# How the first batch's q and k reach the chip: fp32 loads through SyncE and ScalarE, and transposes of two heads at once

## The chip, the cores and the metric

The kernel runs on one core of a Trainium2 chip. The metric is the device time of one execution in microseconds (us); several executions are measured and their median is given. The profile is of one execution, and its "span" is the time from the first to the last instruction in the trace.

The engines are called by their short names: PE (TensorE, the matrix multiplier; "PEld" are its weight loads), DVE (VectorE), ACT (ScalarE), POOL (GpSimd) and SP (SyncE, which only issues transfers here). Each engine works through its own instructions in order. Transfers (DMA) are issued from the queues of POOL, SP or ACT.

## The reference

Sliding-window attention with a linear bias by distance, and behind it a gated feed-forward block. Batch 8, 8 heads, 576 positions, head dimension 64; the inputs are fp32.

```python
scores = scale * np.matmul(q, k.transpose(0, 1, 3, 2))
slopes = 2.0 ** (-8.0 * (np.arange(H) + 1) / H)
bias = slopes[:, None, None] * (-np.abs(rel))[None, :, :]
mask = (rel >= 0) & (rel < 128)
scores = np.where(mask, scores + bias[None], -1e9)
attn = softmax(scores); attn_out = np.matmul(attn, v)
x = attn_out.transpose(0, 2, 1, 3).reshape(B * S, H * D)
out = (gelu(x @ w_gate) * (x @ w_val)) @ w_out
```

## The kernel before, in words

The 4608 tokens go through the feed-forward block in 9 groups of 512 (`gate_val` L465, `out_part` L493); the attention of batch b + 2 is spread over the steps of group g (`todo`, `steps`, L661 to L686). The order on each engine is that of the code. Batches 2 to 7 load q, k and v as bf16 through POOL's queue and are transposed by DMA. Batches 0 and 1 are transposed by PE, since they must be ready early.

**Batch 0** is a prologue written out by hand (L601 to L650).

The loads. `load_runs` (L137) loads q and k so that each partition holds r neighbouring positions of a head (r = 3 for positions 0 to 383, the "first part", on 128 partitions; and for 384 to 575, the "last rows", on 64 partitions, q on partitions 0 to 63 and k on 64 to 127 of one tile, `vb[1]`). The transfers convert fp32 to bf16 on the way and go through POOL's queue. L528 issues heads 0 to 3 of the first part (q, then k), L530 an iota that fills `tmpl` with key minus query distances, L532 heads 4 to 7, L533 the last rows, then v and the weights. POOL has eight completion counters for its transfers, so the ninth waits until the first has landed.

The tables. From `tmpl` DVE makes `ident` (L550, the identity for the transposes), `far` (L552), `tmpl` as distances (L554), `dist` in bf16 (L555), and `slopes` (L561, the identity times each head's slope, in two halves). ACT makes `emask` (L557, eight exps of 128x256, one for each head: the decay by distance); DVE copies parts of it to make the masks of the last blocks (`masks_of_last_blocks`, L578). `sel0`, `sel` and `sel8` select rows to spread the denominators, `ones4` and `ones8` sum them.

The work. `keep_busy(64)` puts 64 matmuls of zeros on PE ahead of the first real one. `first` (L590) transposes two heads of the first part: `transpose_runs` (L151) makes six transposes, one head and 64 columns each, and `untangle` (L162) copies the PSUM result to `qT` or `kT` in the order of positions. `biases0` and `scores0` (L254, L263) add slope times distance and q times k in PSUM, and ACT takes the exp (L209) into P. `rest` (L595) does the same for the last rows, in 12 transposes of 64x64 per call; `scores0_rest` (L273) makes their scores. `sums4` (L340) sums P by head (L364) and takes the reciprocal (L368); `products_first` and `spread_first` (L451, L456) multiply P with v (L431), spread the reciprocals (L378) and write `xT` (L459). `masks` are the products of P with `emask` (L212) that the last rows still need. Then `gate_val` (L473 matmuls, L479 gelu, L480 product) starts, with `sums4(0, 1)`, `spread4` and `values(0, 1)` between.

The buffers that the change uses: `wo`, the output matrix (12 slices of 512 columns), is loaded only at L651, and before that its slices 0 to 2 hold `slopes` and `dist`. The place of the last rows in `vb[1]` is that of batch 1's v, loaded at L654.

Of the kernel before, what the change touches and what calls it, by code (L numbers as in the profile page):

```python
# [7 lines left out]
FP32 = mybir.dt.float32  # L8
BF16 = mybir.dt.bfloat16
AF = mybir.ActivationFunctionType  # L10
# [22 lines left out]
def kernel(  # L33
# [30 lines left out]
    psum = ctx.enter_context(  # L64
        tc.tile_pool(name="psum", bufs=8, space=bass.MemoryType.PSUM))


    heat = [0]

    def bank():  # L70
        ps = psum.tile([128, 512], FP32, name="ps")
        for _ in range(heat.pop()):
            nc.tensor.matmul(out=ps[:, 0:64], lhsT=zeros, rhs=zeros[:, 0:64], start=True, stop=True)
        heat.append(0)
        return ps

    def keep_busy(n):
        heat[0] = n

    wg = consts.tile([128, 4, DFF], BF16, name="wg")  # L80
    wv = consts.tile([128, 4, DFF], BF16, name="wv")
# [55 lines left out]
    def load_runs(b, n, h0, h1):  # L137
        first, parts, r = RUNS[b][n]
        for what, src in ((0, q), (1, k)):
            nc.gpsimd.dma_start(  # L140
                out=runs(what, b, n)[:, h0:h1, :],
                in_=src[b][h0:h1, first:first + parts * r, :].rearrange(
                    "h (p r) d -> p h (r d)", r=r))
# [7 lines left out]
    def transpose_runs(b, n, what, c, ps):  # L151
        first, parts, r = RUNS[b][n]
        src = runs(what, b, n)
        p = 64 * what if (b, n) == (0, 1) else 0
        for x in range(r):
            for i in (0, 1):
                nc.tensor.transpose(  # L157
                    out=ps[64 * i:64 * i + 64, parts * x:parts * x + parts],
                    in_=src[:, 2 * c + i, 64 * x:64 * x + 64],
                    identity=ident[p:p + parts, p:p + parts])  # L160
# [93 lines left out]
    def biases0(cs):  # L254
        pss = []
        for c in cs:
            ps = [bank(), bank()]
            pss.append(ps)
            for i in (0, 1):
                bias(2 * c + i, ps[i], 2)  # L260
        return pss

    def scores0(cs, pss):  # L263
        for c, ps in zip(cs, pss):
            for j, q0, col in ((0, 0, 0), (1, 128, 256)):
                for i in (0, 1):
                    added(c, i, j, q0, 256, ps[i][:, col:col + 256])
        for c, ps in zip(cs, pss):
            for i in (0, 1):
                exp(prob(0)[:, c, i, 0:512], ps[i])  # L270


    def scores0_rest(cs, later):  # L273
        pss = []
        for c in cs:
            ps = [bank(), bank()]
            pss.append(ps)
            for j, q0, n, col in ((2, 384, 128, 0), (3, 384, 192, 128), (4, 512, 64, 320)):
                for i in (0, 1):
                    score(0, c, i, j, q0, n, ps[i][:, col:col + n])  # L280
        P = prob(0)
        for c, ps in zip(cs, pss):
            for i in (0, 1):
                exp(P[:, c, i, 640:1024], ps[i][:, 0:384])
            later.append((P[:, c, :, 640:1024], emask[:, 2 * c:2 * c + 2, 128:512]))
# [38 lines left out]
    def row(b):  # L324
        if b not in sumrow:
            sumrow[b] = r_pool.tile([128, S], FP32, name="r")
            recip[b] = r_pool.tile([128, 4, S], FP32, name="rb")
        return sumrow[b]
# [11 lines left out]
    def sums4(b, s, added=True):  # L340
        first, w, count = shape(b, s)
        ps = bank()
        P, T = prob(b).rearrange("p c i n -> p (c i) n"), both.get(b)
        mms = []
        for h in range(H):
            for x in range(count):
                t = first + w * x
                g, lhsT = ((x, ones4[:, 32 * h:32 * h + 32]) if count == 4 else
                           (2 * x + h // 4, ones8[:, 32 * (h % 4):32 * (h % 4) + 32]))
                if added and t >= 128:  # L350
                    mms.append((g, lhsT, T[:, h, t - 128:t - 128 + w], 0, w))
                elif added:
                    mms.append((g, lhsT, P[:, h, t:t + w], 0, w))
                else:
                    for _, a, e, col in PIECES[min(b, 1)][s]:
                        lo, hi = max(a, t), min(e, t + w)
                        if lo < hi:
                            mms.append((g, lhsT, P[:, h, col + lo - a:col + hi - a],
                                        lo - t, hi - t))

        by_group = [[m for m in mms if m[0] == g] for g in range(4)]
        mms = [ms[n] for n in range(max(map(len, by_group))) for ms in by_group if n < len(ms)]
        for n, (g, lhsT, rhs, lo, hi) in enumerate(mms):
            nc.tensor.matmul(  # L364
                out=ps[32 * g:32 * g + 32, lo:hi], lhsT=lhsT, rhs=rhs,
                start=all(m[0] != g for m in mms[:n]), stop=all(m[0] != g for m in mms[n + 1:]),
                skip_group_check=True)
        nc.vector.reciprocal(row(b)[:, first:first + w], ps[:, 0:w])  # L368
# [82 lines left out]
    def products_first(cs, copies):  # L451
        n = PARTS[0][0][1]
        for c, ps in zip(cs, products(0, 0, cs)):
            copies[c](out=recip[0][:, c, 0:n], in_=ps[:, 0:n])

    def spread_first():  # L456
        w = PARTS[0][0][1] // 4
        for g, ps in enumerate(spread4_banks(0, 0)):
            nc.vector.tensor_tensor(  # L459
                out=xT[:, :, w * g:w * g + w], in0=recip[0][:, :, w * g:w * g + w],  # L460
                in1=ps[:, 0:4 * w].rearrange("p (c x) -> p c x", c=4), op=ALU.mult)
# [63 lines left out]
    tmpl = consts.tile([128, 256], FP32, name="tmpl")  # L525
    far = consts.tile([128, 256], FP32, name="far")
    nc.vector.memset(zeros, 0.0)
    load_runs(0, 0, 0, 4)  # L528

    nc.gpsimd.iota(tmpl, pattern=[[1, 256]], base=0, channel_multiplier=-1,  # L530
                   allow_small_or_imprecise_dtypes=True)
# [9 lines left out]
        nc.vector.memset(slope1[:, h:h + 1], -8.0 * 2.0 ** (-8.0 * (h + 1) / H))  # L541
    nc.vector.memset(ones4, 0.0)
    nc.vector.memset(ones4.rearrange("p (h x) -> p h x", x=36)[:, :, 0:4], 1.0)
    nc.vector.memset(ones8, 0.0)
    nc.vector.memset(ones8.rearrange("p (h x) -> p h x", x=40)[:, :, 0:8], 1.0)
    for t in (kT[0], kT[1]):
        nc.vector.memset(t[:, :, 576:640], 0.0)
    for t in vb:
        nc.vector.memset(t[64:128, 4, :], 0.0)
    nc.vector.tensor_single_scalar(out=ident, in_=tmpl[:, 0:128], scalar=0.0, op=ALU.is_equal)  # L550
    for lo, bound, op in ((0, 0.0, ALU.is_lt), (128, 127.5, ALU.is_gt)):
        nc.vector.tensor_scalar(out=far[:, lo:lo + 128], in0=tmpl[:, lo:lo + 128],  # L552
                                scalar1=bound, scalar2=1e9, op0=op, op1=ALU.mult)
    nc.vector.tensor_tensor(out=tmpl, in0=tmpl, in1=far, op=ALU.max)  # L554
    nc.vector.tensor_copy(out=dist, in_=tmpl)  # L555
    for h in range(H):
        nc.scalar.activation(out=emask[:, h, 0:256], in_=tmpl, func=AF.Exp,  # L557
                             scale=-(2.0 ** (-8.0 * (h + 1) / H)))

    def made_slopes(lo, hi):  # L560
        nc.vector.tensor_tensor(  # L561
            out=slopes[:, lo:hi, :], in0=ident.unsqueeze(1).to_broadcast((128, hi - lo, 128)),
            in1=slope1[:, lo:hi].unsqueeze(2).to_broadcast((128, hi - lo, 128)), op=ALU.mult)

    made_slopes(0, 4)

    load_w(512, 768)
    load_w(768, 1024)
    load_w(1024, 1280)
    for n in (0, 1):  # L570
        load_runs(1, n, 0, 8)
    load_w(1280, DFF)

    nc.vector.tensor_reduce(
        out=sel0, in_=ident.rearrange("p (g h r) -> p h g r", g=4, r=4)[:, :, :, 0],
        op=ALU.add, axis=mybir.AxisListType.X)

    def masks_of_last_blocks(lo, hi):  # L578
        for to, at, n in ((256, 0, 192), (448, 0, 64)):
            nc.vector.tensor_copy(out=emask[:, lo:hi, to:to + n], in_=emask[:, lo:hi, at:at + n])  # L580
# [8 lines left out]

    def first(w, c, copy, ps):  # L590
        ps = ps.bitcast(BF16)
        transpose_runs(0, 0, w, c, ps)
        untangle(copy, 0, 0, w, c, c + 1, ps)

    def rest(w, cs, copy):  # L595
        ps = bank().bitcast(BF16)
        for n, c in enumerate(cs):
            transpose_runs(0, 1, w, c, ps[:, 192 * n:192 * n + 192])
        untangle(copy, 0, 1, w, cs[0], cs[-1] + 1, ps)

    keep_busy(64)  # L601
    held = [bank() for _ in range(4)]
    for c in (0, 1):
        first(0, c, dve, held[c])
    ps0 = biases0((0,))
    masks_of_last_blocks(0, 4)
    for c in (0, 1):
        first(1, c, dve, held[2 + c])
    nc.scalar.copy(out=sel, in_=sel0.unsqueeze(2).to_broadcast((128, 8, 64)))
    made_slopes(4, 8)  # L610
    ps0 += biases0((1,))
    scores0((0, 1), ps0)
    held = [bank() for _ in range(4)]
    for w, c in ((0, 0), (0, 1), (1, 0), (1, 1)):
        transpose_runs(0, 0, w, 2 + c, held[2 * w + c].bitcast(BF16))
# [3 lines left out]
    scores0((2, 3), ps0)  # L619
    ps0 = biases0_2()  # L620
    scores0_2(ps0)
    masks_of_last_blocks(4, 8)
    for cs in ((0, 1), (2, 3)):
        for w in (0, 1):
            rest(w, cs, dve)
    row(0)
    masks = []
    scores0_rest((0,), masks)
    sums4(0, 0, False)
    scores0_rest((1,), masks)  # L630
    products_first(range(4), (act, dve, act, dve))
    spread_first()
    for args in masks:
        mask(*args)
    masks.clear()
# [138 lines left out]
```

## Time and profile before

| what | value |
|---|---|
| median of 4 runs | 353.29 us (353.01 to 354.14) |
| the profiled execution | 354.14 us, of which the span is 352.4 |
| PE busy | 343.8 us, 98% of the span |
| DVE, ACT, POOL busy | 192.9, 178.5, 107.7 us |
| mean granted PE clock | 0.995 of full speed |
| transfers through POOL's queue | 18.88 MB in 109,536 packets |

How to read it: busy time is the time in which an engine had an instruction at work. The chain of work that ended last is followed back from the last instruction of the span: at each step to what released it, so its pieces add up to the span, and a wait in it is a wait of the whole kernel. A row of windows gives a stretch, its length, then for PE, PEld, DVE, ACT and POOL the busy us and the number of instructions, then the granted PE clock, the DMA share and the GB/s moved. A row of the timeline or of groups names the line, the operation, and output and input tiles by name.

### The profile page before, as it was taken

To read this page: it belongs to the slowest core of one execution; us is meant where nothing else is said; L and a number is where in the kernel's file an instruction comes from. 1 tells how busy PE (TensorE), PEld (TensorE's weight loads), DVE (VectorE), ACT (ScalarE), POOL (GpSimd) and SP (SyncE) were. 2 spreads that over 40 slices of the span, in tenths; PEclk is the share of its full clock that TensorE was granted. 3 is DMA by queue.
4 is the path that set the end of the run, shared out by engine and by line. 5 is a ranking of instruction groups with operands and counts; after the bars stand their busy time and mean duration, and the time that the engine had idled before them with its cause. 6 is when DMAs were issued, how large, how long until landed. Compare 5 with 4: busy or idle time off the path is not lost.

```text
span 352.4 us, 6898 instructions
## 1 busy us (share of the span) xinstructions
PE 343.8 (98%) x2788; PEld 171.4 (49%) x2788; DVE 192.9 (55%) x344; ACT 178.5 (51%) x328; POOL 107.7 (31%) x141
## 2 busy tenths in 40 slices
PE   7899999999999999999999999999999999999996
PEld 5565555544455445445444544455444444444444
DVE  7685458443878846766557555745674404403320
ACT  4763476535889365632963287327832133313322
POOL 8874663490950085002910193004000000000000
PEclk9899999999999999999999999999999999999999
DMA  9999999999999199973997499759206020011002
GB/s 97 162 195 191 204 161 181 178 148 190 112 180 152 33 139 189 204 154 63 150 207 157 92 129 207 142 132 97 91 2 136 30 91 1 1 63 58 0 27 94
DMA packets 148800, 42.62 MB, mean 121 GB/s; under 512 B 134776, under 2 KB 141688, under 8 KB 148768
## 3 DMA queue, kind: packets, MB, share of 16 engines
q0 software_dynamic: 109536, 18.88, 69.2%
q1 hardware_dynamic: 36432, 17.31, 20.5%
q10 hardware_dynamic: 2800, 5.99, 8.0%
q8 instruction: 22, 0.36, 0.4%
q14 instruction: 10, 0.08, 0.1%
HBM read 43.65 MB, written 9.53 MB: 151 GB/s over the span
## 4 chain that ended last, share of the span: by engine, by line
PE 90%; DVE 3%; ACT 2%; DMA 2%; POOL 1%; issue 1%; POOLq 0%; ACTq 0%; DVEq 0%
PE ps L473 54%; PE ps L499 24%; PE ps L431 4%; PE ps L205 3%; DMA ks<-in_k_dram 2%; ACT P L209 1%; PE ps L364 1%; PE ps L378 1%; DVE P L212 1%; PE ps L400 1%; PE ps L515 1%; PE ps L157 1%; DVE S L312 1%; POOL qs L140 0%; DVE kT L165 0%
## 5 line engine op out<-in xcount | busy, mean ns | idle before, releaser
L480 DVE TENSOR_TENSOR hT<-ps,gelu 128x512 bf16<-128x512 f32 (+3 forms) x112 | 73.8, 668 | 102.1 <-PE ps L473 96.3
L479 ACT ACTIVATE gelu<-ps 128x512 bf16<-128x512 f32 (+3 forms) x112 | 64.5, 582 | 115.6 <-PE ps L473 110.7
L473 PE MATMUL ps<-xT,wg 128*128 128x512 bf16 (+3 forms) x448 | 112.2, 372 | 1.4 <-DVE xT L459 0.7
L473 PE MATMUL ps<-xT,wv 128*128 128x512 bf16 (+3 forms) x448 | 111.7, 372 | 0.0
L499 PE MATMUL ps<-wo,hT 128*128 128x512 bf16 x420 | 95.6, 380 | 0.0
L209 ACT ACTIVATE P<-ps 128x512 bf16<-128x512 f32 (+1 forms) x130 | 65.9, 614 | 8.6 <-PE ps L205 5.6
L473 PEld LDWEIGHTS <-wv 128*128 128x128 bf16 x448 | 43.4, 98 | 50.4 <-issue 0.3
L473 PEld LDWEIGHTS <-wg 128*128 128x128 bf16 x448 | 42.1, 98 | 50.2 <-issue 2.8
L499 PEld LDWEIGHTS <-hT 128*128 128x128 bf16 x420 | 38.9, 98 | 46.6 <-issue 1.7
L212 DVE TENSOR_TENSOR P<-P,emask 128x1024 bf16<-128x1024 bf16 (+1 forms) x60 | 39.5, 679 | 24.0 <-ACT P L209 23.8
L504 ACT COPY osb<-ps 128x512 f32<-128x512 f32 x32 | 19.2, 599 | 35.5 <-PE ps L499 33.1
L114 POOL DMA_DIRECT2D vb<-in_v_dram x40 | 34.0, 904 | 6.1 <-PE ps L473 2.1
L445 DVE TENSOR_TENSOR xT<-ps,rb 128x320 bf16<-128x320 f32 (+2 forms) x64 | 22.9, 422 | 11.9 <-DMA rb<-rd 5.1
L724 POOL COPY mark<-hT 1x2 bf16<-1x2 bf16 x4 | 0.7, 174 | 92.4 <-DVE hT L480 92.4
L114 POOL DMA_DIRECT2D qs<-in_q_dram x30 | 25.2, 860 | 6.9 <-DMA wo<-in_moe_w_out_dram 5.9
L114 POOL DMA_DIRECT2D ks<-in_k_dram x30 | 25.4, 903 | 3.8 <-DMA qs<-in_q_dram 3.8
L205 PE MATMUL ps<-qT,kT 64*128 64x256 bf16 (+3 forms) x352 | 18.4, 236 | 0.6 <-DVE qT L165 0.3
L405 DVE RECIPROCAL r<-ps 128x256 f32<-128x256 f32 (+1 forms) x10 | 18.8, 1921 | 0.0
L431 PE MATMUL ps<-P,vb 128*64 128x256 bf16 (+3 forms) x384 | 17.6, 239 | 0.0
L431 PEld LDWEIGHTS <-vb 128*64 128x64 bf16 x384 | 14.7, 110 | 5.2 <-issue 4.6
L205 PEld LDWEIGHTS <-kT 64*128 64x128 bf16 x352 | 11.9, 94 | 10.4 <-issue 8.1
L312 DVE TENSOR_TENSOR S<-P 128x1024 bf16<-128x1024 bf16 (+3 forms) x27 | 15.1, 591 | 0.5
(74 smaller groups left out, 137.0 us busy)
## 6 DMA issues: line engine op xcount, KB each, us to landing
out_dram<-osb SPq DMA_DIRECT2D x35, 256.0 KB, 3.0
rb<-rd ACTq DMA_DIRECT2D x10, 576.0 KB, 7.7
vb<-in_v_dram POOLq DMA_DIRECT2D x32, 128.0 KB, 6.5
qs<-in_q_dram POOLq DMA_DIRECT2D x24, 128.0 KB, 4.7
ks<-in_k_dram POOLq DMA_DIRECT2D x24, 128.0 KB, 5.4
wo<-in_moe_w_out_dram POOLq DMA_DIRECT2D x2, 768.0 KB, 15.5
wg<-in_moe_w_gate_dram POOLq DMA_DIRECT2D x5, 256.0 KB, 8.3
wv<-in_moe_w_val_dram POOLq DMA_DIRECT2D x5, 256.0 KB, 8.9
```

Source lines behind the costliest of these rows:

```text
L114: nc.gpsimd.dma_start(out=t[0:n, j, :].rearrange("p (h d) -> p h d", h=H), in_=src[b][:, 128 * j:128 * j + n, :].rearrange("h p d -> p h d"))
L205: nc.tensor.matmul(out=out, lhsT=columns(kT, b, i, c, 128 * j, 128), rhs=rhs, start=True, stop=True)
L209: nc.scalar.activation(out=dst, in_=src, func=AF.Exp, scale=0.125)
L212: nc.vector.tensor_tensor(out=dst, in0=dst, in1=m, op=ALU.mult)
L405: nc.vector.reciprocal(row(b)[:, lo:hi], ps[:, 0:hi - lo])
L431: nc.tensor.matmul(out=ps[64 * i:64 * i + 64, a - lo:e - lo], lhsT=vb[b % 2][:, j, 64 * h:64 * h + 64], rhs=P[:, c, i, col:col + e - a], s ...
L445: nc.vector.tensor_tensor(out=xT[:, c, at:at + e - a], in0=ps[:, a - lo:e - lo], in1=recip[b][:, c, a:e], op=ALU.mult)
L473: nc.tensor.matmul(out=ps, lhsT=w[:, c, 128 * f:128 * (f + 1)], rhs=xT[:, c, t0 + lo:t0 + hi], start=(c == 0), stop=(c == 3))
L479: nc.scalar.activation(out=gl[:, 0:n], in_=pg, func=AF.Gelu)
L480: nc.vector.tensor_tensor(out=hid[g][:, f, lo:hi], in0=pv, in1=gl[:, 0:n], op=ALU.mult)
L499: nc.tensor.matmul(out=acc[g], lhsT=hid[g][:, f, 128 * t:128 * (t + 1)], rhs=wo[:, f, :], start=(f == 0), stop=(f == NF - 1))
L504: (nc.vector.tensor_copy if t == 0 and g < 2 or t == 1 and g == 0 else nc.scalar.copy)(out=osb, in_=acc[g])
```

## The change

For batch 0's first part, heads 0 to 3 no longer come through POOL's queue. Four transfers bring them as fp32: q of heads 0, 1 and 2, 3 through SP's queue, k through ACT's, into a part of `wo` that is still free (`raw`, slices 3 to 8). They are converted to bf16 on the chip, q by DVE and k by ACT (`cast`), and laid out so that two heads stand side by side in 128 columns; one transpose of 128 columns then does two heads (`first`). Untangling is done by DVE for q and by ACT for k.

The last rows still come through POOL's queue, but DVE copies them into such a layout (`pairs1`, slices 9 to 11 of `wo`) before PE transposes them two heads at once, 24 transposes instead of 48.

The filler matmuls are 40 ahead of the first pair of heads and 8 ahead of the second, instead of 64 at the start. The iota becomes POOL's first instruction. Moved to later places: `emask` exps (in groups of 2, 1, 2 and 3 heads), the memsets of `kT`, `vb` and `ones8`, the second half of `slopes`, both calls of `masks_of_last_blocks`, and `sel`; `sel0` moves ahead. Nothing after the prologue is changed, but the load of `wo` (L651 before) now has to wait for what used its slices.

```diff
-    load_runs(0, 0, 0, 4)
+    raw = [wo[:, 3 + 3 * w:6 + 3 * w, :].rearrange("p a x -> p (a x)").bitcast(FP32)
+           for w in (0, 1)]
+    pairs0 = [t[0].rearrange("p j x -> p (j x)")[:, 0:768].rearrange(
+        "p (x c y) -> p x c y", x=3, c=2) for t in (qs, ks)]
+    pairs1 = wo[:, 9:12, :]
+    for h in (0, 2):
+        for w, src, queue in ((0, q, nc.sync), (1, k, nc.scalar)):
+            queue.dma_start(
+                out=raw[w].rearrange("p (h x) -> p h x", h=4)[:, h:h + 2, :],
+                in_=src[0][h:h + 2, 0:384, :].rearrange("h (p r) d -> p h (r d)", r=3))
...
+    def cast(w, c, copy):
+        copy(out=pairs0[w][:, :, c, :].rearrange("p x (i d) -> p x i d", i=2),
+             in_=raw[w].rearrange("p (c i x d) -> p c x i d", c=2, i=2, x=3)[:, c])
...
     def first(w, c, copy, ps):
         ps = ps.bitcast(BF16)
-        transpose_runs(0, 0, w, c, ps)
+        for x in range(3):
+            nc.tensor.transpose(out=ps[:, 128 * x:128 * x + 128], in_=pairs0[w][:, x, c, :],
+                                identity=ident)
         untangle(copy, 0, 0, w, c, c + 1, ps)
 
     def rest(w, cs, copy):
         ps = bank().bitcast(BF16)
+        p = 64 * w
         for n, c in enumerate(cs):
-            transpose_runs(0, 1, w, c, ps[:, 192 * n:192 * n + 192])
+            for x in range(3):
+                nc.tensor.transpose(
+                    out=ps[:, 192 * n + 64 * x:192 * n + 64 * x + 64],
+                    in_=pairs1[p:p + 64, x, 128 * c:128 * c + 128],
+                    identity=ident[p:p + 64, p:p + 64])
         untangle(copy, 0, 1, w, cs[0], cs[-1] + 1, ps)
 
-    keep_busy(64)
     held = [bank() for _ in range(4)]
     for c in (0, 1):
-        first(0, c, dve, held[c])
-    ps0 = biases0((0,))
-    masks_of_last_blocks(0, 4)
-    for c in (0, 1):
-        first(1, c, dve, held[2 + c])
-    nc.scalar.copy(out=sel, in_=sel0.unsqueeze(2).to_broadcast((128, 8, 64)))
+        cast(0, c, dve)
+        if c == 0:
+            decays(0, 2)
+        cast(1, c, act)
+        if c == 0:
+            decays(2, 3)
+        keep_busy(held[2 * c], (40, 8)[c])
+        first(0, c, dve, held[2 * c])
+        first(1, c, act, held[2 * c + 1])
+    ps0 = biases0((0, 1))
+    scores0((0, 1), ps0)
+    decays(3, 5)
     made_slopes(4, 8)
-    ps0 += biases0((1,))
-    scores0((0, 1), ps0)
+    for t in (kT[0], kT[1]):
+        nc.vector.memset(t[:, :, 576:640], 0.0)
+    for t in vb:
+        nc.vector.memset(t[64:128, 4, :], 0.0)
...
     ps0 = biases0_2()
     scores0_2(ps0)
-    masks_of_last_blocks(4, 8)
+    dve(out=pairs1.rearrange("p x (h d) -> p x h d", d=64),
+        in_=vb[1].rearrange("p j x -> p (j x)")[:, 0:1536].rearrange(
+            "p (h x d) -> p x h d", h=H, x=3))
+    masks_of_last_blocks(0, 4)
     for cs in ((0, 1), (2, 3)):
         for w in (0, 1):
             rest(w, cs, dve)
     row(0)
+    nc.vector.memset(ones8, 0.0)
+    nc.vector.memset(ones8.rearrange("p (h x) -> p h x", x=40)[:, :, 0:8], 1.0)
     masks = []
     scores0_rest((0,), masks)
+    nc.scalar.copy(out=sel, in_=sel0.unsqueeze(2).to_broadcast((128, 8, 64)))
     sums4(0, 0, False)
     scores0_rest((1,), masks)
     products_first(range(4), (act, dve, act, dve))
+    decays(5, 8)
     spread_first()
+    masks_of_last_blocks(4, 8)
     for args in masks:
         mask(*args)
```

More of the change, by code (lines that the diff above doesn't have):

```diff
@@ L65, with keep_busy @@
         tc.tile_pool(name="psum", bufs=8, space=bass.MemoryType.PSUM))
-    heat = [0]
     def bank():
-        ps = psum.tile([128, 512], FP32, name="ps")
-        for _ in range(heat.pop()):
+        return psum.tile([128, 512], FP32, name="ps")
+    def keep_busy(ps, n):
+        for _ in range(n):
             nc.tensor.matmul(out=ps[:, 0:64], lhsT=zeros, rhs=zeros[:, 0:64], start=True, stop=True)
[L74 to L78, printed above, removed]
     wg = consts.tile([128, 4, DFF], BF16, name="wg")
@@ L543 @@
     nc.vector.memset(ones4.rearrange("p (h x) -> p h x", x=36)[:, :, 0:4], 1.0)
[L544 to L549, printed above, removed]
     nc.vector.tensor_single_scalar(out=ident, in_=tmpl[:, 0:128], scalar=0.0, op=ALU.is_equal)
@@ L555, with decays @@
     nc.vector.tensor_copy(out=dist, in_=tmpl)
-    for h in range(H):
-        nc.scalar.activation(out=emask[:, h, 0:256], in_=tmpl, func=AF.Exp,
-                             scale=-(2.0 ** (-8.0 * (h + 1) / H)))
+    def decays(lo, hi):
+        for h in range(lo, hi):
+            nc.scalar.activation(out=emask[:, h, 0:256], in_=tmpl, func=AF.Exp,
+                                 scale=-(2.0 ** (-8.0 * (h + 1) / H)))
     def made_slopes(lo, hi):
@@ L563, in made_slopes @@
             in1=slope1[:, lo:hi].unsqueeze(2).to_broadcast((128, hi - lo, 128)), op=ALU.mult)
+    def cast(w, c, copy):
+        copy(out=pairs0[w][:, :, c, :].rearrange("p x (i d) -> p x i d", i=2),
+             in_=raw[w].rearrange("p (c i x d) -> p c x i d", c=2, i=2, x=3)[:, c])
     made_slopes(0, 4)
+    nc.vector.tensor_reduce(
+        out=sel0, in_=ident.rearrange("p (g h r) -> p h g r", g=4, r=4)[:, :, :, 0],
+        op=ALU.add, axis=mybir.AxisListType.X)
     load_w(512, 768)
@@ L572 @@
     load_w(1280, DFF)
-    nc.vector.tensor_reduce(
-        out=sel0, in_=ident.rearrange("p (g h r) -> p h g r", g=4, r=4)[:, :, :, 0],
-        op=ALU.add, axis=mybir.AxisListType.X)
     def masks_of_last_blocks(lo, hi):
```

## The prediction

> **What bounds the kernel now.** I read, in order: busy shares and granted clock, the chain of work that ended last, the timeline of the first 30 us, the landing times of the first transfers, and the busy time in windows of 3.4 us. First the page:
>
> ```profile
> PE 343.8 (98%) x2788; PEld 171.4 (49%) x2788; DVE 192.9 (55%) x344; ACT 178.5 (51%) x328; POOL 107.7 (31%) x141
> PE 90%; DVE 3%; ACT 2%; DMA 2%; POOL 1%; issue 1%; POOLq 0%; ACTq 0%; DVEq 0%
> ```
>
> TensorE is busy 98% of the span and carries 90% of the chain. From 28.02 us on the diff touches nothing that the chain waits for. So the change is worth what it moves the dense stretch, and that is decided before 28 us. In the chain in order of time (start, us, what):
>
> ```profile
> 4.02 6.59 DMA ks<-in_k_dram
> 10.61 0.04 issue
> 10.65 0.53 PE ps L157 x6
> ...
> 14.37 0.56 DVE qT L165
> 14.93 0.48 DVE kT L165
> 15.40 0.04 issue
> 15.45 0.28 PE ps L205 x4
> 15.73 0.89 PE ps L364 x43
> ...
> 28.02 13.42 PE ps L473 x77
> ```
>
> The chain starts in a transfer: k of heads 4 to 7, issued at 4.02, landed at 10.6. Behind it come transposes, untangling copies, scores, the copies of rows 384 to 575 (14.37) and the first denominators (L364). I call the start of L364 S: 15.66 in the timeline.
>
> **Step 1: the transfers.** Issue time plus time to landing gives 4.95 and 7.05 us for q and k of heads 0 to 3, 8.07 and 10.6 for heads 4 to 7, 11.75 and 13.04 for the last rows. The first bytes move at 2.75. Each transfer is 512 runs of 768 B read, so six take 13.04 - 2.75 = 10.3 us: 1.71 each. After the change heads 0 to 3 go through SP and ACT. The nearest row is an output store, issued at 342.11 by SP; the second row below shows it at 328 GB/s from 342.9 on, 0.8 us behind its issue.
>
> ```profile
> 342.10:342.90 0.80, 0.80 (x6) 0.39 (x4) 0.00 (x0) 0.00 (x0) 0.00 (x0) 1.00 0.00 0
> 342.90:343.70 0.80, 0.80 (x6) 0.33 (x5) 0.00 (x0) 0.00 (x0) 0.00 (x0) 1.00 0.88 328
> ```
>
> SP and ACT are free at 0.75, so bytes move from about 1.6, 1.15 us earlier. Four pieces of 196 KB at some 300 GB/s take 2.6 us. Each issue costs its queue 0.6 us (L508, L411); ACT's two push its table load (1.28) from 0.74 to 1.95, ready at 3.25, before which it had only waited for tmpl until 4.67. POOL's queue loses its first two issues (0.90 and 0.77), and the iota goes ahead: its first load starts at about 1.65, first bytes 1.5 us later (as 1.25 to 2.75) at 3.15. By then about 465 of the 786 KB are in; the other 320 delay POOL's four transfers by 1.07. The last k rows land at 3.15 + 4 x 1.71 + 1.07 = **11.1 us**, not 13.04. Bounds: 10.0 without sharing; 11.9 if the six keep 1.71 each from 1.6 on; 13.0 if nothing comes earlier.
>
> The Trainium skill (DMA: Bandwidth & Descriptors, Issuing engines are not separate DMA queues) speaks against this step: several issuing engines save only the issue time, since all run on the same 16 DMA engines. By it the sum would be that of the 11.9 bound.
>
> **Step 2: heads 0 to 3.** The iota now ends near 1.6, not 3.37, so DVE's run from ident to sel0 (3.40 to 5.68, 2.28 us) ends at 3.9; tmpl is ready at 2.85. Casts of 128x384 fp32 are not in the trace: 0.29 for 128x256 (L555) and 0.55 for 384 from PSUM (L454) bound them; I take 0.4 on DVE and 0.45 on ACT (L454 on ACT 0.44). Q is cast at 3.9 to 4.3, k beside it. Three transposes of 128 columns replace six of 64 (12 took 0.53): 0.25. Untangling costs DVE 0.55; on ACT 0.45. The second pair lands at 4.4 to 5.9, its cast starts near 5.2, its transposes end near 6.1. Behind a cast that waits stand, on DVE, the untangling, slopes and memsets, on ACT two decays, and PE waits for both; to 7.6 there is room. Four biases (about 0.22 each) and eight scores end near 7.6; the first exp starts near 7.2 instead of 9.18. ACT now has decays(3,5), 2 x 0.32 on it, where it idled 1.42 before 12.66: four exps to 9.3, decays to 9.9, four exps to 12.0, two to 13.0. Heads 4 to 7 (landing 5.9 and 7.6) are transposed from 7.6 on; made_slopes and the four moved memsets (0.68 + 0.31 + 0.55) fit on DVE from 6.3 to 7.9, and the untangling ends near 10.4 (was 12.7). So S cannot be before **13.05**, ACT's last exp.
>
> **Step 3: the last rows.** These now bound. Before, they had landed at 13.04 and waited for TensorE until 13.95. Now a DVE repack of 128x1536 bf16 stands between, which no row shows. The nearest is L580, 128x768, at 0.284 once and 0.725 once (POOL busy beside it): 0.57 to 1.45; I take 0.75. Behind it on DVE masks_of_last_blocks(0,4) (0.48 or 0.85, I take 0.5) comes before the first untangling; the transposes, 24 instead of 48 (0.69), lie beside it. Untangling starts at 11.1 + 0.75 + 0.5 = 12.35 instead of 14.37, and S = 12.35 + 1.3 = **13.65** (15.66 - 14.37 = 1.3): **2.0 us earlier**. From the bounds: at most 2.6 (the 13.05); with 11.9 and both slow copies S is 15.5, 0.15 earlier; if the rows also came no earlier, it would be 0.95 later.
>
> **Step 4: given back.** sel (0.60) on ACT now stands between the two pairs of L209 exps; ACT is then 0.6 ahead, so nothing; without that lead it delays the spread by 0.3. Decays(5,8), 0.96, fill an idle of 0.94 before L209's last four exps. masks_of_last_blocks(4,8) is moved into the one stretch where DVE has no idle:
>
> ```profile
> 20.00:25.00 5.00, 4.65 (x72) 3.10 (x71) 4.93 (x11) 3.94 (x9) 3.36 (x5) 1.00 1.46 199
> ```
>
> (the third pair, DVE, 4.93 of 5 us). Behind it there wait the four mask products, the second denominators on TensorE and the second reciprocal; the products end at 23.10, TensorE wants them at 23.34. Cost 0.48 - 0.24 = 0.25, or 0.6 with the slow copy and the reciprocal behind; I take **0.4**. The ones8 memsets (0.2) lie in front of the reciprocal while it waits for L364: nothing, 0.2 without. The output matrix's load now also waits for the casts and the repack, done 15 us before: nothing.
>
> If v came late, step 3 would gain less: its third block lands at 7.9 + 7.4 = 15.3, 2.26 behind the last k rows; kept, 13.4, and is used at S + 1.2 = 14.8. Covered.
>
> **Sum.** -2.0 + 0.4 + 0.2 for small waits = **-1.4 us**. The profiled execution took 354.14 (span 352.4, and 1.7 around it), so 352.7 in its terms; the median of the runs shown is 353.29, so **351.9**.
>
> **Rivals.**
>
> *The engines are shared and only the earlier start counts.* Last k rows at 11.9, S 1.2 earlier, 0.4 + 0.05 back: -0.75, 352.55 (at 13.0: +0.35). For: in 2.75 to 13.04 the DMA share is never low. Against: the store above ran at 328 GB/s where the loads move 146 written (292 read). Chance 0.18.
>
> *The clock falls: slower.* Windows of 3.4 us (third to last column the granted clock):
>
> ```profile
> 4.20:7.60 3.40, 1.89 (x35) 1.02 (x33) 3.22 (x9) 2.93 (x9) 3.40 (x5) 1.00 1.43 155
> 7.60:11.00 3.40, 3.10 (x32) 1.49 (x32) 2.09 (x4) 1.96 (x5) 2.81 (x5) 0.50 1.43 144
> 17.80:21.20 3.40, 2.69 (x60) 2.12 (x54) 2.84 (x7) 2.46 (x8) 3.19 (x6) 1.00 1.51 193
> ```
>
> After a window with TensorE busy 56% (1.89) the next ran at half clock; 79% (2.69) left it full. Before, that fell where the chain waited for the transfer. Now the first window (0.8 to 4.2) has 40 of the 64 filler matmuls, 2.2 us: 64%. And in 11.0 to 14.4 I count 0.3 + 0.45 + 0.5 + 0.75 = 2.0 of work: 59%. If a share near 60% halves the clock, the scores come 1 us later (S + 0.4, ACT's exps), and the products and the spread of 14.4 to 17.8 run at 0.85 instead of 0.53 (twelve transposes at the two clocks): + 1.3. Sum -1.4 + 1.7 = **+0.3**, 353.6, up to +1.0. It decides from some 56 to 79% of a window on, wherever the window falls. The Trainium skill (TensorE: Matmul & The Clock Gate, What's actually happening) tells the same of windows that run free of the program; by it the place may differ in each execution. The trace agrees with the 3.4 us. Chance 0.22.
>
> *Something of the first part is late* (fp32 landing, casts behind POOL's transfers, table load), S held by ACT's exps: within 0.5 of before. Chance 0.08.
>
> **How the numbers follow.** Forecast 0.52, with -2.3 to -0.8. 0.3%, 1.06 us, is about what a measurement of this kernel can tell. Faster by more: three quarters of the forecast, 0.39, and 0.03 of the first rival: 0.42. Slower by more: a third of the clock's, 0.07, and 0.03 of the last: 0.10. The rest 0.48. Range 350.7 (S at its bound of 13.05, without the small waits) to 354.0 (beyond the clock's 353.6, and beyond 11.9 with both slow copies: 353.29 - 0.15 + 0.6 = 353.75).
>
> **What would show it.** Landing of the last k rows at 10 to 12 us; the first exp near 7.2; the first untangling of the last rows near 12.4; S near 13.7; TensorE dense from 26.6; the granted clock at 1.00 between S and the spread. Wrong if the repack waits for something other than its transfer, if S follows ACT's exps, or if half clock lies over the products.

## The result, and the profile after

The changed kernel took **354.08 us** (median of 48 runs, 352.89 to 354.80), the kernel before 353.03 (median of 74 runs, 352.46 to 355.86). The ratio of the means is 1.0021, 95% interval 1.0014 to 1.0029: **0.75 us slower**. The forecast was 351.9, and its range ended at 354.0. The medians lie 1.05 apart; the means less, since 17 of the 74 runs of the kernel before lie at 353.8 or more (one cause is told below, under the third experiment).

The profiled execution took 354.25 us, span 352.2. Of its page, the same two lines that the prediction showed of before:

```profile
PE 343.3 (97%) x2736; PEld 171.0 (49%) x2736; DVE 193.7 (55%) x345; ACT 180.2 (51%) x332; POOL 105.8 (30%) x139
PE 91%; ACT 3%; DVE 3%; DMA 1%; issue 0%; ACTq 0%
```

The share of DMA in the chain is halved (k of heads 4 to 7 no longer stands in it). Its chain in order of time (start, us, what):

```profile
0.75 3.20 DMA wo<-in_q_dram
...
3.98 0.67 DVE qs L568
...
6.45 0.82 PE ps L598 x6
7.27 1.71 PE ps L239 x4
8.98 0.97 PE ps L244 x8
...
13.77 0.56 DVE qT L160
14.32 0.48 DVE kT L160
14.80 0.05 issue
14.85 0.29 PE ps L200 x4
15.13 0.91 PE ps L359 x38
...
27.67 13.42 PE ps L468 x77
```

The chain now starts in the first fp32 transfer, goes through the cast and then through TensorE itself: four biases of 1.71 us and eight scores of 0.97. (Lines after the loads are smaller than before: L359 was L364, L468 was L473.) S, the start of L359 in the timeline, is 15.06, only 0.6 earlier than before's 15.66; the dense stretch starts at 27.67 instead of 28.02. The two rows of S, before and after:

```profile
15.66 0.96 PE L364 MATMUL ps<-P,ones 128*32 128x96 bf16 x64
15.06 0.98 PE L359 MATMUL ps<-P,ones 128*32 128x96 bf16 x64
```

What happened to the rest is in the timeline of the changed kernel (start, us, engine, line, operation):

```profile
3.98 0.66 DVE L568 CAST qs<-wo 128x384 bf16<-128x384 f32 x1 [0.65 <-DMA wo<-in_q_dram]
4.32 0.51 ACT L568 CAST ks<-wo 128x384 bf16<-128x384 f32 x1 [0.48 <-DMA wo<-in_k_dram]
...
7.06 1.91 PE L239 MATMUL ps<-wo 128*128 128x512 bf16 x4
...
8.91 1.03 PE L244 MATMUL ps<-qT,kT 64*128 64x256 bf16 x8
...
9.55 2.06 ACT L204 ACTIVATE P<-ps 128x512 bf16<-128x512 f32 x4 [1.76 <-PE ps L244]
...
10.67 1.10 PE L239 MATMUL ps<-wo 128*128 128x512 bf16 x4
...
11.70 0.39 PE L244 MATMUL ps<-qT,kT 64*128 64x256 bf16 x4
...
12.14 0.94 DVE L641 COPY wo<-vb 128x1536 bf16<-128x1536 bf16 x1
13.00 0.60 DVE L585 COPY emask<-emask 128x768 bf16<-128x768 bf16 x2
...
13.77 0.56 DVE L160 COPY qT<-ps 128x384 bf16<-128x384 bf16 x1 [0.17 <-PE ps L607]
```

The same four biases take 1.91 us at 7.06 and 1.10 at 10.67: up to some point between them TensorE ran at half clock. The view of windows of the changed kernel does not tell it:

```profile
0.80:4.20 3.40, 2.32 (x40) 2.16 (x40) 2.57 (x19) 2.01 (x3) 3.19 (x5) 1.00 0.64 186
4.20:7.60 3.40, 2.40 (x22) 1.97 (x23) 2.21 (x5) 2.01 (x5) 3.40 (x5) 1.00 1.49 206
7.60:11.00 3.40, 3.40 (x38) 1.54 (x37) 2.09 (x7) 1.64 (x5) 3.40 (x6) 1.00 2.11 167
...
17.80:21.20 3.40, 2.58 (x58) 2.18 (x55) 2.85 (x6) 3.37 (x10) 2.71 (x4) 1.00 1.45 198
20.00:25.00 5.00, 4.77 (x72) 3.11 (x70) 5.00 (x12) 3.51 (x8) 3.09 (x4) 1.00 1.45 197
```

It prints 1.00 where no clock record lies, and the first clock record of this trace is the rise to 1.00 at 9.85 us. So read the clock from the length of matmuls of one shape, not from that column, in the first microseconds of a program. The first record of the kernel before is a rise too, at 4.18: it also starts at half clock, and the 61 fillers in its window of 0.80 to 4.20 take 3.20 us, about as long for each as the 40 here. Then come the 3.41 us at 0.50 (7.60 to 11.01) that the prediction showed.

### The profile page after: what moved, and what is told of

It is laid out like the page before. It is cut to its first block, busy times and chain, and to the rows that moved or that the text cites. A ratio compares the mean times of both kernels' runs of the same rounds, so it can differ in the third digit from the quotient of the medians.

```text
span 352.2 us, 6808 instructions
## 1 busy us (share of the span) xinstructions
PE 343.3 (97%) x2736; PEld 171.0 (49%) x2736; DVE 193.7 (55%) x345; ACT 180.2 (51%) x332; POOL 105.8 (30%) x139
## 4 chain that ended last, share of the span: by engine, by line
PE 91%; ACT 3%; DVE 3%; DMA 1%; issue 0%; ACTq 0%
PE ps L468 53%; PE ps L494 24%; PE ps L426 5%; PE ps L200 3%; ACT P L204 2%; PE ps L373 1%; DVE P L207 1%; PE ps L359 1%; DMA wo<-in_q_dram 1%; PE ps L395 1%; PE ps L510 1%; DVE S L307 1%; PE ps L239 1%; DVE qT L160 1%; PE ps L152 1%; PE ps L244 0%
## 5 line engine op out<-in xcount | busy, mean ns | idle before, releaser
L468 PE MATMUL ps<-xT,wg 128*128 128x512 bf16 (+3 forms) x448 | 112.2, 372 | 1.3 <-DVE xT L454 0.7
L468 PE MATMUL ps<-xT,wv 128*128 128x512 bf16 (+3 forms) x448 | 111.6, 372 | 0.0
L468 PEld LDWEIGHTS <-wv 128*128 128x128 bf16 x448 | 43.4, 98 | 50.2 <-issue 0.2
L468 PEld LDWEIGHTS <-wg 128*128 128x128 bf16 x448 | 42.1, 98 | 50.1 <-issue 2.5
L200 PEld LDWEIGHTS <-kT 64*128 64x128 bf16 x352 | 11.9, 94 | 10.5 <-issue 8.1
```

The source lines that it names most:

```text
L200: nc.tensor.matmul(out=out, lhsT=columns(kT, b, i, c, 128 * j, 128), rhs=rhs, start=True, stop=True)
L468: nc.tensor.matmul(out=ps, lhsT=w[:, c, 128 * f:128 * (f + 1)], rhs=xT[:, c, t0 + lo:t0 + hi], start=(c == 0), stop=(c == 3))
```

## The experiments

**Theory:** TensorE starts every execution at half clock and is raised only at the end of a stretch of 3.41 us in which it was busy enough (the stretch at 0.50 in before is 3.41 us long, and the clock records of all these traces, but for the last of each, are 3.41 us or a multiple of it). The 40 fillers (2.32 us) fill no such stretch, the 64 of before did (TensorE busy 3.18 us of the 3.41 ahead of its rise at 4.18); the loss is the fillers'. **Rival:** the change gains nothing by its own steps (casts, repack, DVE's order), whatever the clock.

**1. The changed kernel with more fillers.**

```diff
-        keep_busy(held[2 * c], (40, 8)[c])
+        keep_busy(held[2 * c], (64, 18)[c])
```

> The changed kernel with 64 filler matmuls ahead of the first pair of heads and 18 ahead of the second, not 40 and 8. Theory A (the clock): in the profile of the changed kernel four biases of 512 columns took 1.91 us at 7.06 and eight scores 1.03 at 8.91, twice the time of the same forms later, so TensorE ran at half clock from before 4.7 until about 9.9, because it stood idle from 3.3 to 4.7. With the gap filled the biases take about 1.0 and the scores 0.55, S comes 1.2 to 1.8 us earlier, and the time falls by 0.8 to 1.6 us, to 352.5 to 353.3. Theory B (the data: fp32 landing at 3.95 and 4.25, casts of 0.66 behind them, and not the clock): the fillers change nothing beyond 0.2 us.

Measured: 352.88 us (12 runs) beside 352.97 for the kernel before, ratio 1.0000 (0.9985 to 1.0015). Its timeline:

```profile
1.00 3.32 PE L73 MATMUL ps<-zeros 128*128 128x64 bf16 x64 [1.00 <-DVE zeros L522]
...
6.80 1.03 PE L239 MATMUL ps<-wo 128*128 128x512 bf16 x4
...
8.18 2.07 ACT L204 ACTIVATE P<-ps 128x512 bf16<-128x512 f32 x4 [0.70 <-PE ps L244]
...
13.72 1.23 PE L359 MATMUL ps<-P,ones 128*32 128x96 bf16 x64
```

The clock rises at 3.86, the biases take 1.03 instead of 1.91, S is 13.72 (1.34 earlier) and the dense stretch starts at 26.15 (1.52 earlier). The median falls by 1.2 us (354.08 to 352.88), inside the 0.8 to 1.6 that was expected, and the loss against the kernel before is gone. But no gain over it is left either: the theory holds for the loss, and the rival for nearly all of the gain that had been forecast.

**2. No fillers** (`(0, 0)` in the same place).

> The changed kernel without any filler matmul. Theory A: the 40 and 8 fillers do not keep the clock up as it is, so without them the half clock is there from the first transpose too and lasts as long or one window longer; the time is the same or up to 1.5 us longer, 354.1 to 355.6. Theory B: without fillers nothing changes, or the 0.1 us that they stand in the way are won: 354.0 to 354.1.

Measured: 355.14 us (7 runs), ratio 1.0069 (1.0039 to 1.0099), as expected. The execution that was profiled is the slowest of the seven, 357.44. There the clock rises at 12.56 only and falls again from 22.80 to 26.22; L359 starts at 15.91, most of it at 16.40, and the dense stretch at 30.83. Such a fall lowers the mean clock of an execution to 0.995 (half of 3.41 us in 352); three of the seven runs show that, and the median one does not. The transposes start at 4.69 as with 40 or 64 fillers, so the fillers hold nothing up. Fewer fillers, later clock, later S.

**3. The kernel before with 40 fillers** (`keep_busy(40)` instead of 64), and **the kernel before itself**, looked at once more.

> The kernel before with 40 fillers instead of 64. Theory A: the first window is as idle as in the changed kernel and half clock comes earlier; but there the chain waits for k of heads 4 to 7 at 10.6 us, which hides most: 0 to 0.6 us slower than before. Theory B: no difference.

Measured: 353.57 us, ratio 1.0014 (1.0003 to 1.0026), within the theory's 0 to 0.6; clock up at 10.17, S 14.93, dense from 27.29. The clock's price is there without the change as well (0.6 beside 352.97). But S is *earlier* than in the trace of before that the prediction worked from (15.66), with fewer fillers. So that trace needed a second look:

> The kernel before, unchanged, for a second look. The prediction was summed against one profiled execution of 354.14 us, while most executions of it take 352.5 to 353.3. Theory C (the profiled execution was a late one): here k of heads 4 to 7 lands about 1 us earlier than 10.6 and S is at 14.5 to 14.9, not 15.66; the span is near 351.2. Rival (the excess lies around the span or behind 28 us): S is again at 15.6.

Neither forecast: the one execution took 354.2 us, another late one. k of heads 4 to 7 landed at 9.6, 1.0 earlier than in the first trace, and yet S was 15.67. The clock had fallen for 3.41 us from 7.44, and the chain runs through TensorE at half clock (start, us, what):

```profile
2.14 5.25 DMA ks<-in_k_dram
...
7.44 0.85 PE ps L157 x12
8.29 0.96 PE ps L244 x2
9.25 0.97 PE ps L249 x8
```

Side by side with the other profiles of kernels that share the order of before and its 64 fillers or more (experiments 4 and 5; times in us, S is the start of the first denominators):

| profile | first rise | TensorE busy in the 3.41 us behind it | clock after that | k of heads 4 to 7 landed | S |
|---|---|---|---|---|---|
| before | 4.18 | 56% | 0.50 for 3.41 us | 10.6 | 15.66 |
| b_again | 4.03 | 44% | 0.50 for 3.41 us | 9.6 | 15.67 |
| x4 | 4.25 | 49% | 0.50 for 3.41 us | 9.9 | 15.55 |
| y_mid | 4.08 | 52% | 0.50 for 3.41 us | 9.4 | 15.34 |
| y_sp | 4.68 | 67% | 1.00 | 9.1 | 14.07 |
| x8 | 5.10 | 75% | 1.00 | 9.0 | 14.04 |
| b_fill | 5.81 | 98% | 1.00 | 9.2 | 14.08 |

S goes with the clock: 15.3 to 15.7 with the fall, 14.04 to 14.08 without. The fall comes behind the emptier stretches, and what empties them is the wait for k of heads 0 to 3. This k landed at 7.0 to 7.4 in the four with the fall and at 6.0 to 6.8 in the three without, and the stretch begins at another point in each; which counts for more the runs do not separate.

The trace that the prediction worked from is late in a second way too. Its k of heads 4 to 7 landed later than in all the others, and its chain, as the prediction showed, begins with that landing, not with TensorE: of what follows, only the 0.36 us up to 11.01 ran at half clock. So in that execution the landing alone would have kept S near 15.4 (an estimate from this chain). With the clock full, in y_sp, the chain to S comes through no transfer: it starts in the iota (2.97) and goes through DVE's tables, its untangling (5.66 and 7.36) and its masks (6.59). So a usual execution has S near 14.05 and the dense stretch from 26.4 to 26.8; this is read from y_sp and x8, as both profiles of the kernel before itself are late ones.

Not every late run has the fall. Of the 93 runs of the kernel before that were timed in these experiments, 6 took 353.8 us or more; two of them have a mean clock of 0.995, the other four 0.999 or 1.00. A late first rise would leave no mark there, since no record lies ahead of it; whether it was that is open. For the 17 of the 74 no clock is on record.

**4. What remains at equal clock.** Four and eight tiny transfers (64 bytes, half from SP, half from ACT) ahead of all else in the kernel before, to ask whether early transfers alone cost time:

> The kernel before with four tiny transfers (64 bytes each, two on SP's and two on ACT's queue) at its start, whose data nobody uses. In the changed kernel 0.2 us more lie between ACT's last copy and the span's end (2.84 against 2.65), and 0.25 more around the span (2.03 against 1.78). Theory D (transfers from SP and ACT take eight completion counters in turn; four more move the last output transfer from the eighth counter to the fourth, and the end of the program goes through the counters in order): both the 0.2 and the 0.25 appear here. Theory E (the size or the data of the four fp32 transfers): neither appears.

> As x4, with eight tiny transfers: the last output transfer is on the eighth counter again. Theory D: 2.65 and 1.78 us, as before. If any early transfer from SP or ACT brings the two costs: 2.84 and 2.03, as with four.

Measured: 352.98 us, ratio 1.0011 (1.0000 to 1.0021), and 353.03, 1.0006 (0.9994 to 1.0018). Two costs show that no engine's row has. First, the time outside the span (the time less the span, mean of the runs): 1.78 to 1.82 in the kernel before, 1.975 with four and with eight, 2.01 in the changed kernel. Second, the end of the span behind ACT's last copy: 2.65 us before, 2.89 in the changed kernel, 2.92 with four transfers, 2.66 with eight. A reading of the program, which no view shows, is that the completion counters of these transfers are taken in turn, eight of them, so that four transfers more put the last output transfer on the fourth instead of the eighth. Tested in the changed kernel with 64 and 18 fillers, with four more transfers much later:

```diff
+        if g == 3:
+            for n in range(4):
+                nc.sync.dma_start(out=far[0:1, 16 * n:16 * n + 16], in_=q[0][0, n:n + 1, 0:16])
```

> The changed kernel with 64 and 18 fillers, and four tiny transfers on SP's queue in the middle of the kernel, whose data nobody uses, so that the last output transfer is on the eighth counter. Theory D: 0.4 us less than with the fillers alone: 352.45, and 0.1 to 0.2% faster than before. Otherwise 352.9, as with the fillers alone.

Measured: 352.52 us, near the 352.45 expected, but with a ratio of 0.9995 (0.9985 to 1.0005) the gain of 0.1 to 0.2% is not shown; the end is 2.65 again, the time outside stays at 2.005. So the end goes with the count of transfers, 0.24, as the reading has it. For the other 0.2, the kernel before with eight tiny transfers from SP alone, at the start or in the fourth group:

> The kernel before with eight tiny transfers of 64 bytes from the queue of SyncE alone, ahead of all else. Four and eight tiny transfers from SyncE and ScalarE put 0.2 on the time outside the span (time less span 1.975, against 1.78 to 1.79 in the kernel before). If any early transfer from such a queue does it: 1.95 to 2.0 again. If it is ScalarE's queue, which in the kernel before issues its first transfer much later: 1.78 to 1.80.

> The kernel before with eight tiny transfers of 64 bytes from the queue of SyncE, issued in the fourth group (some 100 us on) and not at the start. With eight of them at the start from SyncE alone the time less the span was 1.97, as with ScalarE's, against 1.79 in the kernel before. If only a transfer in the first microseconds adds these 0.2: 1.78 to 1.80 again. If it is the count of transfers that such a queue carries, wherever they stand: 1.95 to 2.0.

Measured: outside the span 1.97 at the start, 1.82 in the middle (kernel before on the same chip 1.81). It is a transfer from SP or ACT in the first microseconds that adds 0.15 to 0.2 here, not ACT's queue and not the count. By what means is open. The times themselves, 352.75 (ratio 1.0000, 0.9990 to 1.0010) and 352.74 (0.9998, 0.9974 to 1.0022), cannot show so little.

**5. The kernel before with an early clock, and the changed one with still more fillers.**

> The kernel before with 70 fillers instead of 64, and 20 more matmuls of 64 columns ahead of k's first transposes, so that its TensorE clock is raised early and is not lowered again. Theory that the changed kernel lost by the half clock alone and has a gain of its own at equal clock (last row of S 13.72 and dense part 26.15 in the changed kernel with 64 and 18 fillers, against 14.04 and 26.80 in the kernel before with eight tiny transfers, whose clock stayed full): this one stays at S 14.0 to 14.3 and the dense part at 26.8, its span at 351.0 to 351.2, and its time at 352.8 to 353.0, like the kernel before, because most executions of the kernel before keep the full clock anyhow. Rival, that the kernel before also loses by its clock in most executions: 352.0 to 352.5, and the change itself is then worth nothing or less at equal clock.

Measured: 353.58 us, ratio 1.0037 (1.0019 to 1.0055): neither forecast. In the trace the clock rose at 5.81 and stayed, S was 14.08, as expected (two of the ten runs show a mean clock of 0.995 all the same). But then its timeline has this:

```profile
18.39 0.47 PE L378 MATMUL ps<-r,sel 32*128 32x96 f32 x7 [0.91 <-issue]
```

TensorE stood for 0.91 us and waited for nothing that the profile shows; a 16 KB packet of the kind "instruction" had ended 1.47 us before TensorE went on. Stops of 0.51 (x8), 0.55 (e7_no_repack) and 0.57 (e2_nofill) end 1.2 to 1.5 behind such a packet. Traces without a stop, that of y_sp for one, have such packets too. That the added instructions move TensorE's code loading is a guess, and was not tested. As a price of the change at equal clock this run is of no use; its S is.

> The changed kernel with 70 and 20 fillers and four tiny transfers late, so that the last output transfer is again the eighth in its rotation. Theory that 64 fillers are already enough to raise the clock and the first fp32 pair only lands at 4.2: the same as with 64 and 18, 352.4 to 352.6 (0.3 to 0.45 below the kernel before). Rival, that 64 are too few in some executions (its profiled one rose only at 6.5): 352.2 to 352.4. Rival, that the fillers themselves now hold up the first transposes: 352.6 to 352.9.

Measured: 352.78 us, ratio 1.0001 (0.9991 to 1.0010), in the range that the last rival gave for fillers that hold up the transposes. In the trace they do: the first transpose starts at 4.92, not 4.69. But it costs nothing, for the biases start at 6.80 and S is 13.72 as with 64 and 18; the dense stretch starts at 26.45 and not at 26.15, mostly for a stop of 0.20 at 20.60 like those above. More than 64 and 18 fillers gain nothing.

**6. Without the repack**, the last rows transposed one head at a time as before (48 transposes instead of 24), the rest as in the run of e5:

```diff
-    dve(out=pairs1.rearrange("p x (h d) -> p x h d", d=64),
...
-            for x in range(3):
-                nc.tensor.transpose(
...
+            transpose_runs(0, 1, w, c, ps[:, 192 * n:192 * n + 192])
```

> The changed kernel with 64 and 18 fillers and four tiny late transfers, but without the repack: the last rows of q and k are transposed from where they landed, one head at a time, 48 transposes of 64 columns as in the kernel before instead of 24. The prediction put the repack on the path at 0.75 and took the halved transposes to give back 0.4 to 0.9. Theory that the repack and the masks behind it lie beside the scores of the first rows on TensorE: TensorE has 24 more transposes of about 0.1, so the last row of S comes 0.3 to 0.8 later and the time is 352.6 to 353.1. Rival, as the prediction had it: without 0.75 of repack ahead of them the last transposes start earlier, and the time is the same or up to 0.3 lower, 352.2 to 352.5.

Measured: 352.82 us, ratio 1.0006 (0.9994 to 1.0018), beside 352.78 with the repack (and 70 and 20 fillers) on the same chip. The timeline without repack:

```profile
12.15 0.69 PE L152 MATMUL ps<-ident,vb 64*64 64x64 bf16 x48
12.56 0.56 DVE L160 COPY qT<-ps 128x384 bf16<-128x384 bf16 x1 [1.28 <-PE ps L152]
```

and with it (70 and 20 fillers):

```profile
10.80 0.94 DVE L641 COPY wo<-vb 128x1536 bf16<-128x1536 bf16 x1
...
12.05 0.59 PE L607 MATMUL ps<-ident,wo 64*128 64x64 bf16 x24
12.42 0.56 DVE L160 COPY qT<-ps 128x384 bf16<-128x384 bf16 x1 [0.28 <-PE ps L607]
```

The last transposes start when TensorE has done the scores of the first part, at 12.15 or 12.05, repack or not. So the repack is hidden, as the theory had it, but the halved transposes bring the first untangling and S forward by 0.14 only (13.86 to 13.72), where the theory gave 0.3 to 0.8. In the time nothing of either shows.

## Why the prediction was wrong

**The step that failed is the clock, and with it the reference.** The prediction read the 40 fillers as 64% of a window, in a TensorE that it took to be at full clock, and asked whether it would *fall*; so it priced half clock as a rival at +0.3, with a chance of 0.22. That rival named the 40 fillers, but it took only 0.4 of S for it and put the rest, 1.3, on the products and the spread. In the changed kernel the clock was never full ahead of 9.85, and was full over the products; that costs 1.34 in S and 1.52 at the dense stretch (e1_fill against after). The Trainium skill (TensorE: Matmul & The Clock Gate, What's actually happening) states that the clock is at half by default and rises after a busy window of about 3.4 us; the trace agrees (rises at 3.86 with 64 fillers, 9.85 with 40, 12.56 with none). The prediction had used the page's free-running window and not its default.

The other half of the same step is "the median of the runs shown is 353.29", to which the profiled 354.14 was moved by a constant. The 0.85 was no constant. It was lateness in the very stretch that the change works on: a k that landed at 10.6, where the other profiles of that order have 9.0 to 9.9, and a half clock window from 7.60 to 11.01. The forecast took its gain from there. Of the 2.0 by which S was to come earlier, a usual execution has 1.6 already (15.66 against 14.05). Against y_sp, which keeps the clock, the change with 64 fillers brings S from 14.07 to 13.72 and the dense stretch from 26.43 to 26.15: **0.3 us** between these two traces, not 1.4. By the timed runs it is 0.3 to 0.5: e6_fill_more and e5_fill_tail are 0.1 and 0.3 below the kernel before (352.78 beside 352.88, 352.52 beside 352.84), and 0.2 of what they gain is spent outside the span.

Point by point:

- *Step 1, transfers: right in sign, and the landing lies outside its bounds.* The last k rows landed at 9.66 (issued 3.66, 6.0 to landing), forecast 11.1, bounds 10.0 to 13.0. In the view of transfers of after, 0 to 16 us in 40 slices:

```profile
GB/s 0 0 0 0 35 84 186 355 367 369 364 271 181 180 183 194 188 181 193 185 193 182 165 156 152 156 153 158 164 180 177 180 178 179 177 201 147 151 160 185
```

  355 to 369 GB/s move from 2.8 to 4.4, nearly all of it the fp32 transfers'; the loads through POOL then run at 150 to 200. Two terms of the sum were off and nearly made up for each other: POOL's first packets move at 4.2 and not 3.15, and from there the four take 5.4 us, about 1.35 each and not 1.71. By the Trainium skill (DMA: Bandwidth & Descriptors, Issuing engines are not separate DMA queues) other issuing engines save only the issue time, which the prediction put at 11.9; the trace does not agree with that time. But here the kind of transfer changed with the queue, from converting to not, and POOL's transfers hardly ran beside the fp32 ones: those were fast and nearly through first. The earlier landing changed nothing, since the rows then wait for TensorE. And part of it was the reference again: in y_sp and b_again these rows land at 11.1 and 11.7, not 13.04.
- *Step 2, heads 0 to 3: the term that binds, mis-sized.* The first fp32 pair landed at 3.95 and 4.25, where the casts were to start at 3.9 with sel0; casts took 0.66 and 0.69 on DVE and 0.51 on ACT (forecast 0.4 and 0.45). The first exp was to be at 7.2: 8.18 at full clock, 9.55 in the changed kernel. The bound "S cannot be before ACT's last exp", 13.05, was the right kind of bound: in e1_fill the chain runs through ACT's exps, four and then six, and most of the matmuls that S begins wait for the last of them:

```profile
8.19 2.06 ACT P L204 x4
...
11.04 3.04 ACT P L204 x6
14.09 0.04 issue
14.13 0.82 PE ps L359 x32
...
26.15 1.55 PE ps L468 x22
```

- *Step 3, last rows: wrong place.* "These now bound" did not hold. The repack took 0.94 (forecast 0.75) and the masks 0.60, but both lay beside the first part's scores; that S at 13.65 was nearly met in e1_fill (13.72), by another path, is luck, and in the changed kernel it was 15.06.
- *Step 4, given back: too much.* masks_of_last_blocks(4, 8) cost its slow 0.83 at 20.63, yet from S to the dense stretch it is 12.61 us, against 12.36 before and 12.43 in e1_fill: 0.07 to 0.25, forecast 0.4 and 0.2 more for small waits, for which the prediction gave no row.
- *Not in the sum:* 0.24 at the end of the span and about 0.2 outside it, both from four transfers more on these queues. Between the two profiled executions they account for what the earlier start does not bring: the dense stretch starts 0.35 earlier, the span is only 0.12 shorter (352.36 to 352.25), and the time is 0.11 longer.

In all, against a usual execution of before: -0.3 to -0.5 by the change's own steps, +0.24 and +0.2 by its transfers, +1.2 by the clock (354.08 less 352.88): +1.1 to +1.3 worked out. The medians are 1.05 apart, and 1.2 if the runs of before of 353.8 and more are left out (352.87). The intervals of the ratios, some 0.1% or 0.35 us, are wider than what is left.

No version tried beats the kernel before beyond its interval; the best was the changed kernel with 64 and 18 fillers and the last transfer back on the eighth counter, at 0.9995 (0.9985 to 1.0005).

## What to carry to other kernels

Before a profile is used as the base of a sum, ask whether its execution is a usual one: place its time among the runs, and if it is a late one, price the late part by itself and do not let the change take credit for it. Matmuls that warm TensorE have a job that is counted in time, not in number: whoever shortens the wait behind them must still fill most of one stretch of 3.4 us (here 84% was enough and 79% was not), and sees whether it did by the length of the first real matmuls. A step that is made faster ahead of a busy engine is worth only the lead that this engine can use: here the last rows landed 3.4 us earlier than in one trace of before and 1.4 earlier than in y_sp, and 0.3 was left of it.

## What the runs showed of the hardware

- TensorE began every profiled execution at half clock, and the rise came at 3.86 to 6.34 us in the eleven profiles of kernels with 64 or more fillers; with 40 (2.32 us) only when real work had filled a stretch, at 9.85 and 10.17.
- Cut into stretches of 3.41 us that end at the first rise, the traces have it behind a stretch in which TensorE was busy 84% or more, and not behind one of 79% or less. Once the clock was full it fell behind stretches of 44 to 62% and behind none of 63% or more.
- In the changed kernel transfers of 192 KB in fp32 from SP's and ACT's queues land 3.2 and 3.5 us after issue; POOL's converting transfers of the same size, issued from 1.35 on, move their first packets at 4.2 and take 5.1 to 6.0 from issue to landing.
- Transfers from such a queue in the first microseconds add 0.1 (e7_no_repack, 1.90 in its profile) to 0.2 us outside the span. Four transfers more on these queues add 0.24 to 0.28 at its end (after, x4), eight more add nothing (x8, e5_fill_tail); by what means they cost it is open.
